# Early expert tiles chosen after four blocks instead of five, five of them instead of three, and the first expert weights loaded one block earlier

## The chip, the cores and the metric

One NeuronCore of a Trainium2 chip. The time is device microseconds from the start to the end of one execution. Five engines run their own instruction queues in order: TensorE (PE, with its weight loads as PEld), VectorE (DVE), ScalarE (ACT), GpSimd (POOL) and SyncE (SP, which here only issues DMAs).

## The reference

Three stages follow one another. A state-space attention over 4 x 8 sequences of 768 steps gives 3072 tokens of 256 values. A dense feed-forward layer (256 to 2048, leaky ReLU, back to 256) follows. Then each token goes to one of eight experts:

```
logits = x @ w_gate + modality_bias[modality_id]
e_idx = np.argmax(logits, axis=1)
...
gate_w = probs[np.arange(N), e_idx]
for e in range(E):
    mask = e_idx == e
    ...
    h = np.maximum(x[mask] @ w1[e], 0.0)
    out[mask] = gate_w[mask, None] * (h @ w2[e])
```

w1[e] and w2[e] hold 256 x 1024 and 1024 x 256 float32 values, 1 MB each. With the inputs that the reference draws, argmax gives all 3072 tokens to one expert: 2048 after four blocks of 512 tokens, 2560 after five. The dense layer's weights come as float64.

## The kernel before, in words

Every float32 matrix product is made of three fp32r products: each operand is split into a rounded part and a rest (hi, lo), and hi x hi, hi x lo and lo x hi are added. A split of weights is a cast on ACT and a subtraction on DVE or POOL (`split`, L531).

**Dense stage.** The tokens come in six blocks of 512. A block has 16 slots; in each, `mm1` makes one 128-row piece of the hidden layer (6 matmuls `h`), ACT, DVE, ACT, DVE make `sa`, `gg`, `gh`, `gl` from it, and `mm2` two slots later adds that piece to the block's output (6 matmuls `y`). Attention of later chunks, the conversion of the float64 weights (`load_win`, `load_wout`, `split_win`, `split_wout`, through the three 8 KB buffers of the pool `rawp`) and the routing of the block before are hung on slots with `at(slot, fn, ...)`. Slot 16j + f is piece f of block j, and L = 80 is the first slot of the last block (block 5). Offsets come from the dictionary Q.

**Routing.** For each block, three slots into the next one: `logits`, `ranks` (four indirect DMAs on POOL scatter the tokens' numbers into the list `il` in DRAM, ordered by expert), `rows` and `rows_out` (the block's output rows go to `yx` in DRAM). `ranks` also adds the block's counts to `base`.

**Expert stage.** It works in tiles of 256 tokens of one expert. For a tile, `m2_idx` (L802) reads its position from a table into an SP register, loads 256 token numbers (`gi`, a DMA on SP) and gathers their rows with two indirect DMAs on POOL (`xg`). `m2_w` (L790) reads the expert's number into an SP register and issues four DMAs of 512 KB on SP (r1: two halves of w1, L794; r2: two of w2, L797). `m2_split1` and `m2_split2` split r1 and r2 (four ACT casts; three DVE subtractions and one on POOL), `m2_xT` transposes and splits the gathered rows, `m2_mm1` makes `hp` (48 matmuls) and `hh`, `hl`, `m2_mm2` makes `o` (48 matmuls) and scatters the rows to the output (POOL).

The first EARLY = 3 tiles are taken from the counts after five blocks (`table_early`, L762, slot L + 5): only full tiles, so that later tokens change nothing in them. Their gathers read `yx` up to the start of the last block. The other tiles come from the final counts (`table_final`, L774), after the last block. 12 tiles run without condition; more stand under conditions that this input never meets.

**Buffers.** The attention's tiles and `rawp` are given back at slot L (`to_late`, L977). Only then are `raw2` (two r1, two r2, four xg) and `wp2` (the first tile's split weights) there.

**Order.** After the last block the list `fin` (L1006) holds: evict_y, logits, m2_xT(1), ranks, table_final, rows twice, m2_mm1(0), rows_out, m2_split1(1). Then for each tile i: m2_mm1(i), m2_xT(i+1), m2_split1(i+1), [m2_idx(i+2)], m2_w(i+2), m2_mm2(i), m2_split2(i+1); m2_idx stands there for tiles from EARLY on. A planner orders the instructions of each engine when the program is built, from its own estimate of when each can start (`schedule_with_timeline_sim=True`, L1070); instructions named in Q's 'pin' stay behind the instruction traced before them on their engine.

Of the kernel before, what the change touches and what calls it, by code (L numbers as in the profile page):

```python
# [8 lines left out]
F32 = mybir.dt.float32  # L9
# [15 lines left out]
Q = {'sg': (0, 1),  # L25
 'i00': 0,
 'i01': 1,
 'lo1': -1,
 'o00': 0,
 'o01': 4,  # L30
 'i10': 3,
 'i11': 3,
 'xe': 2,
# [11 lines left out]
 'rk': 3,  # L45
 'r0': 6,
 'r1': 6,
 'te': 5,
 'ix': 7,
 'w0': 5,  # L50
 'w1': 6,
 's1': 13,
 's2': 13,
 'xt': 14,
 'bt': 4,
 'cv': 2,
# [48 lines left out]
def kernel(  # L105
# [18 lines left out]
    NT, DM = out.shape  # L124
    DFF = w_in.shape[1]
    NE, _, F2 = w1.shape
    P = 128
    NCB = S // P
    NCH = NT // P
    NF = DFF // P  # L130
    NF2 = F2 // P
    T = 256
    KMAX = NT // T
    EARLY = 3
    NFIN = KMAX + NE - 1 - EARLY
    NSTAT = KMAX - EARLY
    YW = DM + 8
    W64 = w_in.dtype == mybir.dt.int64
    blocks = [(i * 512, 512) for i in range(NT // 512)]
# [4 lines left out]
    gp = ctx.enter_context(tc.tile_pool(name="gp", bufs=8))  # L144
    yp = ctx.enter_context(tc.tile_pool(name="yp", bufs=2))
    sp = ctx.enter_context(tc.tile_pool(name="sp", bufs=2))
    psh = ctx.enter_context(tc.tile_pool(name="psh", bufs=2, space=PSUM))
    psy = ctx.enter_context(tc.tile_pool(name="psy", bufs=2, space=PSUM))
    pscb = ctx.enter_context(tc.tile_pool(name="pscb", bufs=2, space=PSUM))
# [4 lines left out]

    early_ctx = ExitStack()
    ap_ = early_ctx.enter_context(tc.tile_pool(name="ap_", bufs=2))
    rawp = early_ctx.enter_context(tc.tile_pool(name="rawp", bufs=3))

    class Pinned:

# [65 lines left out]
    done = cst.tile([1, NE], F32, name="done")  # L226
    tabe = cst.tile([1, 2, EARLY], I32, name="tabe")
    tabf = cst.tile([1, 2, NFIN], I32, name="tabf")
# [506 lines left out]
    def pick(cum, m, tab, dn):  # L735
        sh = [1, m, NE]
        cb = cum.unsqueeze(1).to_broadcast(sh)
        le = sp.tile([1, NFIN, NE], F32, tag="le", name="le")[:, 0:m, :]
        v.tensor_tensor(out=le, in0=cb, in1=tio[:, 0:m].unsqueeze(2).to_broadcast(sh), op=ALU.is_le)
        et = sp.tile([1, NFIN], F32, tag="et", name="et")[:, 0:m]  # L740
        v.tensor_reduce(out=et, in_=le, axis=AX.X, op=ALU.add)
        v.tensor_scalar(out=et, in0=et, scalar1=float(NE - 1), scalar2=None, op0=ALU.min)
        v.tensor_tensor(out=le, in0=le, in1=cb, op=ALU.mult)
        kt = sp.tile([1, NFIN], F32, tag="kt", name="kt")[:, 0:m]
        v.tensor_reduce(out=kt, in_=le, axis=AX.X, op=ALU.max)
        v.tensor_tensor(out=kt, in0=tio[:, 0:m], in1=kt, op=ALU.subtract)
        if dn is not None:
            v.tensor_tensor(
                out=le, in0=ev[0:1].unsqueeze(1).to_broadcast(sh), in1=et.unsqueeze(2).to_broadcast(sh), op=ALU.is_equal
            )  # L750
            v.tensor_tensor(out=le, in0=le, in1=dn.unsqueeze(1).to_broadcast(sh), op=ALU.mult)
            dt = sp.tile([1, NFIN], F32, tag="dt", name="dt")[:, 0:m]
            v.tensor_reduce(out=dt, in_=le, axis=AX.X, op=ALU.add)
            v.tensor_tensor(out=kt, in0=kt, in1=dt, op=ALU.add)
        v.tensor_scalar(out=kt, in0=kt, scalar1=0.0, scalar2=float(KMAX - 1), op0=ALU.max, op1=ALU.min)
        vb = sp.tile([1, NFIN], F32, tag="vb", name="vb")[:, 0:m]
        v.tensor_scalar(out=vb, in0=et, scalar1=float(NT), scalar2=None, op0=ALU.mult)
        v.scalar_tensor_tensor(out=vb, in0=kt, scalar=float(T), in1=vb, op0=ALU.mult, op1=ALU.add)
        v.tensor_copy(tab[:, 0, :], et)
        v.tensor_copy(tab[:, 1, :], vb)  # L760

    def table_early():  # L762
# [6 lines left out]
        v.tensor_tensor(out=done, in0=nf, in1=cum, op=ALU.subtract)  # L769
        v.tensor_scalar(out=done, in0=done, scalar1=float(EARLY), scalar2=0.0, op0=ALU.add, op1=ALU.max)  # L770
        v.tensor_tensor(out=done, in0=done, in1=nf, op=ALU.min)
        pick(cum, EARLY, tabe, None)

# [14 lines left out]
    late = {}  # L788

    def m2_w(i, tab, k):  # L790
        ei = nc.values_load(tab[:, 0, k:k + 1], engines=[ENG.SP], min_val=0, max_val=NE - 1, skip_runtime_bounds_check_because=WHY)
        r1 = late["raw2"].tile([P, 2, F2], F32, tag="r1", name="r1")
        for k in range(2):
            nc.sync.dma_start(out=r1[:, k, :], in_=w1[bass.ds(ei, 1), k * P:(k + 1) * P, :].rearrange("o p f -> p (o f)"))  # L794
        r2 = late["raw2"].tile([P, NF2, DM], F32, tag="r2", name="r2")
        for k in range(2):
            nc.sync.dma_start(  # L797
                out=r2[:, 4 * k:4 * k + 4, :], in_=w2[bass.ds(ei, 1), k * 4 * P:(k + 1) * 4 * P, :].rearrange("o (k p) f -> p (o k) f", p=P)
            )
        m2.setdefault(i, {}).update(r1=r1, r2=r2)  # L800

    def m2_idx(i, tab, k):  # L802
        vi = nc.values_load(tab[:, 1, k:k + 1], engines=[ENG.SP], min_val=0, max_val=NE * NT - T, skip_runtime_bounds_check_because=WHY)
        gi = sp.tile([P, 2], I32, tag="gi", name="gi", bufs=6)
        r = nc.sync.dma_start(out=gi, in_=il[bass.ds(vi, T), :].rearrange("(q p) o -> p (q o)", p=P))
        for w in puts:
            tc.add_manual_dep(
                r.ins, w.name, mybir.DependencyInfo(mybir.DependencyClass.Sync, mybir.DependencyReason.DATA),
                reason="the list read here",
            )  # L810
        lim = blocks[-1][0] if tab is tabe else NT + 1
        xg = late["raw2"].tile([P, 2, YW], F32, tag="xg", name="xg", bufs=4)
        for q in range(2):
            g.indirect_dma_start(
                out=xg[:, q, :], out_offset=None, in_=yx[0:lim, :],
                in_offset=IndirectOffsetOnAxis(ap=gi[:, q:q + 1], axis=0), bounds_check=lim - 1, oob_is_err=False,
            )
        m2.setdefault(i, {}).update(gi=gi, xg=xg)
# [117 lines left out]
    def at(slot, fn, *args):  # L936
        sched.setdefault(max(slot, 0), []).append((fn, args))
# [37 lines left out]
    L = NF * (nb - 1)  # L975

    def to_late():  # L977
        early_ctx.close()
        late["wp2"] = ctx.enter_context(tc.tile_pool(name="wp2", bufs=2))
        late["raw2"] = ctx.enter_context(tc.tile_pool(name="raw2", bufs=2))  # L980

    at(L, to_late)
    at(L + Q["te"], table_early)
    for i in range(EARLY):
        at(L + Q["ix"], m2_idx, i, tabe, i)
    at(L + Q["w0"], m2_w, 0, tabe, 0)
    at(L + Q["w1"], m2_w, 1, tabe, 1)
    at(L + Q["s1"], m2_split1, 0)
    at(L + Q["s2"], m2_split2, 0)
    at(L + Q["xt"], m2_xT, 0)  # L990

    for j in range(nb):
# [20 lines left out]
    for i in range(len(tl)):  # L1013
        if i:
            run(m2_mm1, (i,), "L_")
            if i + 1 < len(tl):
                run(m2_xT, (i + 1,), "L_")
                run(m2_split1, (i + 1,), "L_")
        if i + 2 < len(tl):
            if i + 2 >= EARLY:  # L1020
                m2_idx(i + 2, *tl[i + 2])
            m2_w(i + 2, *tl[i + 2])
        run(m2_mm2, (i,), "L_" if i + 1 < len(tl) else "Z_")
        if i + 1 < len(tl):
            run(m2_split2, (i + 1,), "L_")
    u = nc.values_load(tabu, min_val=0, max_val=NFIN, skip_runtime_bounds_check_because=WHY)

    def cond(k):
        if k >= NFIN:
            return  # L1030
        with tc.If(u > k):
            i = EARLY + k
            m2_idx(i, tabf, k)
            m2_w(i, tabf, k)
            m2_split1(i)
            m2_split2(i)
            m2_xT(i)
            m2_mm1(i)
            m2_mm2(i)
            cond(k + 1)  # L1040
# [34 lines left out]
```

## Time and profile before

| | us |
|---|---|
| three timed runs | 578.73, 585.75, 586.8 |
| their median | 585.75 |
| the profiled execution's own time | 582.59 |
| its span, first to last instruction | 580.7 |
| PE busy | 535.6 (92%) |
| DVE, ACT, POOL busy | 366.2, 334.2, 196.8 |
| mean granted TensorE clock | 0.941 |

The rows further down come from the profiled execution. Times in them are microseconds from the start of its span. A granted clock of 1.00 is 2.4 GHz. "DMA share" is the mean busy share of the 16 DMA engines. In a chain of waits each piece is followed back to what released it. In a timeline row the bracket tells how long the engine stood idle before the instruction and what ended that.

### The profile page before, as it was taken

To read this page: it belongs to the slowest core of one execution; us is meant where nothing else is said; L and a number is where in the kernel's file an instruction comes from. 1 tells how busy PE (TensorE), PEld (TensorE's weight loads), DVE (VectorE), ACT (ScalarE), POOL (GpSimd) and SP (SyncE) were. 2 spreads that over 40 slices of the span, in tenths; PEclk is the share of its full clock that TensorE was granted. 3 is DMA by queue.
4 is the path that set the end of the run, shared out by engine and by line. 5 is a ranking of instruction groups with operands and counts; after the bars stand their busy time and mean duration, and the time that the engine had idled before them with its cause. 6 is when DMAs were issued, how large, how long until landed. Compare 5 with 4: busy or idle time off the path is not lost.

```text
span 580.7 us, 9512 instructions
## 1 busy us (share of the span) xinstructions
PE 535.6 (92%) x3411; PEld 430.4 (74%) x3411; DVE 366.2 (63%) x698; ACT 334.2 (58%) x699; POOL 196.8 (34%) x183
## 2 busy tenths in 40 slices
PE   6999959999999999999999999938987899999991
PEld 3435636678786878788778777826986899999991
DVE  6647998867667776775666665536575266645540
ACT  6427656766666686756765744334435367656640
POOL 5544787710201220013101100205063555456531
PEclk9558998999999999999999999989989799999996
DMA  8995630412243287322510100589008767676300
GB/s 196 143 249 126 189 109 5 100 11 54 34 93 85 46 51 97 78 32 25 119 46 2 39 1 1 21 192 297 20 22 187 251 217 230 225 234 219 114 20 21
DMA packets 128311, 61.01 MB, mean 105 GB/s; under 512 B 84545, under 2 KB 120514, under 8 KB 128258
## 3 DMA queue, kind: packets, MB, share of 16 engines
q1 hardware_dynamic: 125186, 53.94, 41.2%
q0 software_dynamic: 3072, 6.41, 3.3%
q8 instruction: 29, 0.48, 0.4%
q14 instruction: 24, 0.20, 0.2%
HBM read 53.73 MB, written 6.60 MB: 104 GB/s over the span
## 4 chain that ended last, share of the span: by engine, by line
PE 69%; issue 8%; DMA 8%; DVE 6%; POOL 4%; ACT 3%; POOLq 0%; SPq 0%; DVEq 0%; ACTq 0%
PE h L169 19%; PE y L169 18%; PE o L169 8%; PE hp L169 7%; PE psy L169 5%; PE cb L169 4%; DMA r<-in_moe_w_dram 3%; DMA il<-ids,pi 2%; DMA xg<-yx,gi 1%; PE bc L169 1%; DVE lb L169 1%; POOL out_dram L169 1%; PE ps L169 1%; DVE hb L169 1%; PE pb L169 1%
## 5 line engine op out<-in xcount | busy, mean ns | idle before, releaser
L169 ACT CAST gh<-gg 128x512 fp32r<-128x512 f32 x96 | 59.5, 620 | 65.5 <-DVE gg L169 65.4
L169 PE MATMUL h<-xh,wih 128*128 128x512 f32 x192 | 79.2, 416 | 10.6 <-DVE gg L169 10.4
L169 DVE TENSOR_TENSOR gl<-gg,gh 128x512 fp32r<-128x512 f32 x80 | 57.7, 721 | 41.4 <-ACT gh L169 41.2
L169 DVE TENSOR_TENSOR gg<-sa,h 128x512 f32<-128x512 f32 x96 | 65.5, 682 | 22.8 <-ACT sa L169 21.5
L169 PE MATMUL y<-gl,woh 128*128 128x512 f32 x192 | 77.9, 406 | 1.9 <-DVE gl L169 1.7
L169 PE MATMUL h<-xh,wil 128*128 128x512 f32 x192 | 76.4, 398 | 1.0 <-POOL wil L169 1.0
L169 PE MATMUL h<-xl,wih 128*128 128x512 f32 x192 | 76.5, 399 | 0.0
L169 POOL TENSOR_SCALAR_AFFINE_SELECT e<-e 128x1024 f32<-128x1024 f32 (+1 forms) x28 | 30.0, 1075 | 137.2 <-DMA e<-cumd 72.7
L169 PE MATMUL y<-gh,wol 128*128 128x512 f32 x192 | 76.3, 398 | 0.0
L169 PE MATMUL hp<-x2h,w1s 128*128 128x256 f32 x384 | 72.6, 286 | 0.0
L169 PE MATMUL o<-w2s,hh 128*128 128x256 f32 x384 | 71.1, 290 | 0.0
L169 PE MATMUL y<-gh,woh 128*128 128x512 f32 x192 | 65.0, 406 | 5.4 <-ACT gh L169 5.4
L169 ACT ACTIVATE sa<-h 128x512 f32<-128x512 f32 x96 | 57.2, 595 | 21.1 <-PE h L169 18.3
L169 DVE SCALAR_TENSOR_TENSOR hl<-hp,hh 128x512 fp32r<-128x512 f32 x48 | 33.2, 691 | 54.5 <-ACT hh L169 52.4
L169 PEld LDWEIGHTS hp<-x2h,w1s 128*128 128x128 f32 x384 | 61.9, 195 | 0.1
L169 PEld LDWEIGHTS o<-w2s,hh 128*128 128x128 f32 x384 | 60.1, 197 | 0.0
L169 POOL DMA_INDIRECT il<-ids,pi x24 | 25.0, 1040 | 101.2 <-DVE pi L169 50.4
L169 PE MATMUL hp<-x2l,w1s 128*128 128x256 f32 x192 | 54.2, 288 | 0.0
L169 PEld LDWEIGHTS h<-xh,wih 128*128 128x128 f32 x192 | 36.7, 192 | 23.0 <-DVE gg L169 14.0
L169 ACT ACTIVATE hh<-hp 128x512 fp32r<-128x512 f32 x48 | 28.6, 598 | 41.7 <-PE hp L169 36.3
L169 PE MATMUL o<-w2s,hl 128*128 128x256 f32 x192 | 51.9, 287 | 0.0
L169 ACT ACTIVATE e<-e,ncum 128x128 f32<-128x128 f32 x160 | 51.2, 395 | 0.0
(206 smaller groups left out, 1035.5 us busy)
## 6 DMA issues: line engine op xcount, KB each, us to landing
r<-in_moe_w_dram SPq DMA_DIRECT2D x48, 512.0 KB, 5.2
e<-cumd SPq DMA_DIRECT2D x20, 512.0 KB, 7.6
raw<-in_moe_w_in_dram SPq DMA_DIRECT2D x4, 1024.0 KB, 5.5
raw<-in_moe_w_out_dram SPq DMA_DIRECT2D x4, 1024.0 KB
yx<-ysb SPq DMA_DIRECT2D x6, 528.0 KB
xt<-in_x_dram SPq DMA_DIRECT2D x24, 128.0 KB, 4.0
ct<-in_C_dram SPq DMA_DIRECT2D x24, 64.0 KB, 4.6
bt<-in_B_dram SPq DMA_DIRECT2D x24, 64.0 KB
```

The lines of the kernel that those rows point to most:

```text
L169: r = f(*args, **kw)
```

## The change

It does the following.

- EARLY goes from 3 to 5. The two tables change size with it: tabe holds 5 tiles, tabf 14 instead of 16; 12 tiles still run without condition (5 + 7).
- `table_early` and `m2_w` of tile 0 move from slot L + 5 to slot L - 16 + 3 + 1 = 68, in block 4, right behind `ranks` of block 3. The early table is so made from four blocks' counts, and the early gathers read `yx` only up to the start of block 4's rows (`blocks[-2]`).
- The pool `rawp` lives to the end. r1 and r2 no longer have buffers of their own (two each in raw2) but take turns in rawp's three. r1 of tile i + 2 so waits for the split of r2 of tile i, and r2 of tile i + 2 for the split of r1 of tile i + 1; before, r1 and r2 of tile i + 2 waited for the split of r1 and of r2 of tile i.
- `m2_idx` of the early tiles (five now) moves from slot L + 7 to L + 1. xg gets six buffers instead of four.
- The split of tile 0's r1 moves from L + 13 to L + 4, that of r2 from L + 13 to L + 6. `m2_w` of tile 1 moves from L + 6 to L + 9. `m2_xT` of tile 0 stays at L + 14.

```diff
@@
- 'te': 5,
- 'ix': 7,
- 'w0': 5,
- 'w1': 6,
- 's1': 13,
- 's2': 13,
@@
-    EARLY = 3
+    EARLY = 5
@@
+    rawp = ctx.enter_context(tc.tile_pool(name="rawp", bufs=3))
@@
-    rawp = early_ctx.enter_context(tc.tile_pool(name="rawp", bufs=3))
@@ def m2_w(i, tab, k):
-        r1 = late["raw2"].tile([P, 2, F2], F32, tag="r1", name="r1")
+        r1 = rawp.tile([P, 2, F2], F32, tag="raw", name="r1")
...
-        r2 = late["raw2"].tile([P, NF2, DM], F32, tag="r2", name="r2")
+        r2 = rawp.tile([P, NF2, DM], F32, tag="raw", name="r2")
@@ def m2_idx(i, tab, k):
-        lim = blocks[-1][0] if tab is tabe else NT + 1
-        xg = late["raw2"].tile([P, 2, YW], F32, tag="xg", name="xg", bufs=4)
+        lim = blocks[-2][0] if tab is tabe else NT + 1
+        xg = late["raw2"].tile([P, 2, YW], F32, tag="xg", name="xg", bufs=6)
@@
+    at(L - NF + Q["rk"] + 1, table_early)
+    at(L - NF + Q["rk"] + 1, m2_w, 0, tabe, 0)
     at(L, to_late)
-    at(L + Q["te"], table_early)
     for i in range(EARLY):
-        at(L + Q["ix"], m2_idx, i, tabe, i)
-    at(L + Q["w0"], m2_w, 0, tabe, 0)
-    at(L + Q["w1"], m2_w, 1, tabe, 1)
-    at(L + Q["s1"], m2_split1, 0)
-    at(L + Q["s2"], m2_split2, 0)
+        at(L + 1, m2_idx, i, tabe, i)
+    at(L + 4, m2_split1, 0)
+    at(L + 6, m2_split2, 0)
+    at(L + 9, m2_w, 1, tabe, 1)
     at(L + Q["xt"], m2_xT, 0)
```

## Rows read from the trace of the kernel before

**Rows 1.** The page: PE's busy tenths in 40 slices of 14.5 us.

```profile
PE   6999959999999999999999999938987899999991
```

**Rows 2.** Busy by stretch: us, PE, PEld, DVE, ACT, POOL, granted clock, DMA share, GB/s.

```profile
300.00:360.00 60.00, 60.00 (x366) 47.14 (x355) 38.22 (x86) 34.30 (x77) 4.23 (x4) 1.00 0.04 10
...
378.00:396.30 18.30, 7.59 (x18) 4.78 (x19) 7.91 (x7) 7.15 (x10) 2.36 (x1) 0.81 0.90 233
...
423.50:431.00 7.50, 5.93 (x43) 5.64 (x43) 5.85 (x23) 1.66 (x3) 6.12 (x6) 0.77 0.10 35
...
452.50:457.50 5.00, 4.95 (x24) 4.98 (x25) 0.00 (x0) 0.41 (x1) 2.04 (x2) 0.50 1.05 372
457.50:545.00 87.50, 87.50 (x732) 87.50 (x732) 52.21 (x60) 57.19 (x83) 47.73 (x36) 1.00 0.66 213
```

**Rows 3.** The chain that ended last (start, us, what).

```profile
372.60 18.50 DMA r<-in_moe_w_dram
...
396.46 1.36 PE h L169 x6
...
431.79 9.12 DMA il<-ids,pi
...
444.79 7.62 DMA xg<-yx,gi
...
461.30 5.76 PE hp L169 x48
...
473.24 5.76 PE hp L169 x48
479.44 5.76 PE o L169 x48
```

**Rows 4.** SP's timeline around the first expert weights.

```profile
370.43 0.72 SPq L794 DMA_DIRECT2D r<-in_moe_w_dram  x2
...
434.50 0.37 SPq L724 DMA_DIRECT2D yx<-ysb  x1
```

**Rows 5.** ACT's timeline: first and last cast of tile 0's split.

```profile
381.25 1.04 ACT L169 CAST w1s<-r 128x1024 fp32r<-128x1024 f32 x1 [8.58 <-DMA r<-in_moe_w_dram]
...
391.12 1.05 ACT L169 CAST w2s<-r 128x1024 fp32r<-128x1024 f32 x1 [1.31 <-DMA r<-in_moe_w_dram]
```

**Rows 6.** PE's timeline: the first hp matmul of tile 2.

```profile
440.00 0.28 PE L169 MATMUL hp<-x2h,w1s 128*128 128x256 f32 x1
```

**Rows 7.** DVE's timeline: first and last of table_early's 18 instructions.

```profile
365.48 0.24 DVE L169 TENSOR_TENSOR cm<-base,thr 1x96 f32<-1x96 f32 x1
...
370.77 0.16 DVE L169 CAST tabe<-vb 1x3 int32<-1x3 f32 x1
```

**Rows 8.** POOL's and DVE's timelines: POOL's part of tile 0's split, and `gl`.

```profile
392.31 2.36 POOL L169 TENSOR_TENSOR w2s<-r,w2s 128x1024 fp32r<-128x1024 f32 x1 [20.47 <-DMA r<-in_moe_w_dram]
...
392.72 2.50 DVE L169 TENSOR_TENSOR gl<-gg,gh 128x512 fp32r<-128x512 f32 x1 [1.65 <-ACT gh L169]
...
396.50 0.69 DVE L169 TENSOR_TENSOR gl<-gg,gh 128x512 fp32r<-128x512 f32 x1 [0.69 <-ACT gh L169]
```

**Rows 9.** Timelines of SP, DVE, POOL and ACT in the even part of the expert stage.

```profile
465.67 0.98 SPq L797 DMA_DIRECT2D r<-in_moe_w_dram  x2
467.60 0.38 SPq L805 DMA_DIRECT2D gi<-il  x1
...
469.14 2.36 DVE L169 TENSOR_TENSOR w1s<-r,w1s 128x1024 fp32r<-128x1024 f32 x2
...
472.84 1.05 POOL L169 DMA_INDIRECT xg<-yx,gi  x1 [4.68 <-DMA gi<-il]
...
475.24 2.40 POOL L169 TENSOR_TENSOR w2s<-r,w2s 128x1024 fp32r<-128x1024 f32 x1
...
481.89 2.01 ACT L169 CAST w2s<-r 128x1024 fp32r<-128x1024 f32 x2
```

**Rows 10.** The tile r (raw expert weights): time of its 48 DMAs from issue to landing.

```profile
DMA to landing us min/median/max: 3.8/5.2/19.0
```

## The prediction

> **What bounds the kernel now.** I read the page's slices first. PE is at 9 tenths almost everywhere; the reader is to see the 3 in the 27th slice (377 to 392 us) and the 8, 9, 8, 7, 8 behind it [rows 1]. PE sets the time, and what can be won cheaply lies where it stands still. The busy times by stretch show how still: in 300 to 360 PE is busy 60.00 of 60 us at clock 1.00, in 457.5 to 545 it is busy 87.50 of 87.50; from 378.0 to 396.3 it has 18 matmuls in 18.3 us, and the stretches from 423.5 and 452.5 run at granted clocks of 0.77 and 0.50 [rows 2]. The chain that ended last says what PE waited for: a DMA of expert weights for 18.50 us from 372.60, and later the list's scatter (9.12 us from 431.79) and the gather (7.62 us from 444.79) [rows 3].
>
> *First hole.* SP issues the weights of tiles 0 and 1, 4 MB, one behind the other from 370.43 [rows 4]. ACT stands in front of tile 0's first cast until 381.25 and begins the last at 391.12 [rows 5]; the dense stage's `sa` and `gh` are queued behind these casts, and PE behind them. Six matmuls take 1.36 us at the even pace [rows 3], so the 18 in this stretch need 4.1 us: 18.3 - 4.1 = **14.2 us lost**.
>
> *Second hole.* Tile 3 is the first from the final table. `m2_mm1` of tile 2 begins at 440.00 [rows 6], that of tile 3 at 461.30, that of tile 4 at 473.24 [rows 3]. An even tile is 473.24 - 461.30 = 11.94 us; from tile 2 to tile 3 it is 21.3. **9.4 us lost**, partly idle, partly at the clock of 0.50 (1.2 of 2.4 GHz) that PE has from 452.5, when it resumes [rows 2].
>
> *A third dent*, 423.5 to 431: 7.50 - 5.93 = 1.57 us idle and a clock of 0.77 [rows 2], at most 1.57 + 0.23 x 7.5 = 3.3 us. There block 5's routing is mixed with tile 1's split.
>
> **The change part by part.** *Weights of tile 0, slot L + 5 to 68.* The register read and four DMAs (2 MB) move 17 slots ahead, at least 17 x 2 x 1.36 = 46 us, so from 370.43 to about 325 on SP [rows 4]. On SP's queue they pass block 4's `rows_out` and the early gi loads; none of these waits for them. The DMA share in 300 to 360 is 0.04 [rows 2], and 2 MB is half of what took 18.5 us, so they land by about 336. The split at L + 4 and L + 6 comes some 7 slots (20 us) ahead of the old hole, near 355. The 14.2 us go; next in line there is PE itself, as in the stretches beside it. If the cover were gone (weights issued as late as 345), ACT would wait again, a few us.
>
> *table_early with it.* 18 small DVE instructions, from 365.48 to 370.77 between others [rows 7], some 3 us of work, move from block 5 into block 4. There DVE has 38.2 of 60 us busy and PE never waits [rows 2]. Bounds 0 to 3; I take 0.
>
> *Tile 0's split at L + 4 and L + 6.* Four casts of 1.05, three DVE subtractions of 1.2, one on POOL of 2.36, during which `gl` on DVE takes 2.50 instead of 0.69 [rows 5, 8]. They now fall among running slots, beside logits, ranks and rows of block 4. The two slots between `mm1` and `mm2` are 4 x 1.36 = 5.4 us for a chain of four instructions of some 0.7 us [rows 8], so about 2.5 us of delay at a time are hidden. Bounds 0 (all hidden) and 6 (4.2 of casts and 1.8 of `gl` shown in full); I take +1.0, near the lower, since block 4 carries as much for attention (ACT 34.3, DVE 38.2 of 60) at no cost [rows 2].
>
> *m2_idx of five tiles at L + 1.* Five gi DMAs on SP, ten gathers on POOL, two in 2.4 us [rows 9], ahead of block 4's four scatters. The rows and list entries they read are those of blocks 0 to 3, written long before. POOL has 4.2 of 60 us busy [rows 2]; nothing waits for the scatters behind them until table time. Cost 0, at most a delay of those scatters by 12 us, which their list, read after the last block, has to spare.
>
> *m2_w of tile 1, L + 6 to L + 9.* Four DMAs behind `rows_out` of block 4. w1 goes into the third buffer, w2 waits for the split of tile 0's r1. Its split comes only after the last block, behind m2_mm1(0), some 30 us later; five times the landing time [rows 10]. Cost 0.
>
> *Five early tiles.* Tiles 3 and 4 need no final table. Tile 5 does, 2 x 11.94 = 24 us later than tile 3 did, where 9.4 were lost, so those go. Next late is tile 5's gather: gi is read behind tile 4's w2, gathered some 10 us later and lands 5 to 8 us ahead of its transposes.
>
> *Three weight buffers instead of four: the added wait.* In the even part w1's split ends at 469.14 + 2.36 = 471.5; w2's DMAs of the next tile now go out there. Before, w2 went 12 us earlier, at 465.67 for a cast at 481.89 [rows 9]. With 0.9 us to issue and 5.2 to land [rows 10] it is there at 477.6, 4 us early. Behind this wait on SP stand the next gi and w1: gi moves from 467.60 to about 473.4, so its gather on POOL, which started 5.24 us after it, from 472.84 to about 478.7 [rows 9]. The trace shows no such loop. From below 0 (POOL's subtraction goes first: casts end near 472, gather after it, 24 us ahead of use; PE full). From above: the gather keeps its place ahead of the subtraction, which then ends near 483.5 instead of 477.6 [rows 9], while `o` starts at 479.44 [rows 3] and needs it after 12 of its matmuls, at 480.9: 2.6 us for each of seven gathered tiles, 18 us. I take 0: the planner's order follows readiness, and the casts are ready 6 us before the gather would be. The same order decides for tile 2's w2. Should it stand behind block 5's `rows_out` (434.50 [rows 4], 420.3 without the first hole), it lands at 420.3 + 0.9 + 5.2 = 426.4 [rows 9, 10]. Tile 2's `hp` is due at 440.00 - 14.2 = 425.8 [rows 6] and the cast of w2 some 3 us before (481.89 against `hp` near 485.2, after the 48 `o` from 479.44 [rows 3, 9]): 3 to 4 us late.
>
> *Third dent.* Its program order is not touched; I leave it. Bounds: gain 3.3, loss 0.
>
> *Smaller tables, six xg buffers:* 0.
>
> Sum: 580.7 - 14.2 - 9.4 + 1.0 = 558.1 us span, and 1.9 around it (582.59 - 580.7): 560.0. The profiled execution lies 3.2 under the median of the runs and 1.2 under their mean (583.8), so I add 1: **561 us**, 3.7% under the profiled time.
>
> **The rivals.**
>
> *A: the tile loop waits, clock kept (11%).* Both holes go, but each gathered tile waits 2.6 us at POOL's subtraction: 560 + 18 = 578. For it: gather ahead of subtraction is POOL's order now [rows 9]. Against: that order came from a gi ready early, and in the change it is not.
>
> *B: the same loop with the clock (7%), slower than before.* In the dent 1.57 us of idling go with a granted clock of 0.77 over 7.5 us [rows 2], 1.7 us more. If every wait of 2.6 brought some 2 us of low clock, seven tiles cost 7 x 4.6 = 32: 592, slower by 1.6%. It outweighs the two holes from a wait of about 3.4 us per tile in all. The Trainium skill ("TensorE: Matmul & The Clock Gate", "HAM oscillation — how this bites in real kernels") describes this form: a kernel that waits once in every tile starts each tile at the low clock. [...]
>
> *C: one hole in part (10%).* Tile 2's w2 behind `rows_out`: 3 to 4 us idle and as much at the low clock, 567. That the change fails to do what it says (weights still late in block 5) would leave 560 + 14 = 574; I see no way to it but an SP queue held until 345, and count it here.
>
> *Forecast (72%):* both holes gone, 553 to 567.
>
> **How the numbers follow.** A measurement of this kernel tells about 2% from no change, so faster means under 571. Forecast and C are faster: 0.82. A is within 2%, and of B 0.04: 0.15. The rest of B, with a dearer wait, is slower by over 2%: 0.03. Range: from 552 (the dent gone too, 560 - 3.3, and runs 4 us under the profile as the lowest was) to 578, which holds C and half of A.
>
> **What would show it.** r's DMAs from L794 near 320 to 330, ten gathers near 350 to 365; ACT's casts `w1s` without a wait for r; PE full at clock 1.00 from 378 to 396; no `xps` waiting for `xg`; an even tile still 11.94 us from `hp` to `hp`. Wrong if `o` or PEld waits for POOL's `w2s` in each tile, if ACT waits for r in the expert stage, or if PE in block 5 shows idle time before `y` for `gh` or `gl`.

## The result and the profile after

| | before | after |
|---|---|---|
| runs side by side, us | 578.73, 585.75, 586.8, 583.09 | 558.4, 560.86, 562.31, 562.98 |
| their median | 584.42 | 561.59 |
| profiled execution's own time | 582.59 | 558.4 |
| its span | 580.7 | 556.7 |
| mean granted TensorE clock | 0.941 | 0.966 |

The ratio is 0.9615, with a 95% interval of 0.9531 to 0.9699: faster, by 3.9%. The ratios, here and in the table of experiments, leave out runs that fell in a slower state of the chip (one of early3's four, some of the runs of before); the medians hold all runs. The 561 forecast lies 0.6 below the median. The profiled execution of after is the fastest of its four runs, so a few of the 24.0 us between the two profiles are not the change's; they are found below.

In the code of after the helper that records every instruction is L163 (L169 before), and SP issues r1, r2, gi and the block's rows from L788, L791, L799 and L718 (L794, L797, L805 and L724 before).

The page of after, PE's busy tenths in 40 slices:

```profile
PE   7979959999999999999999999999989999999991
```

The 3 of [rows 1] is gone; what is left of the sag is one 8 in the 30th slice. The same table by stretch as in [rows 2], of after:

```profile
300.00:360.00 60.00, 60.00 (x347) 47.63 (x346) 40.45 (x103) 33.76 (x74) 14.13 (x14) 1.00 0.50 100
...
378.00:396.30 18.30, 18.30 (x95) 15.57 (x95) 9.39 (x14) 7.59 (x13) 0.00 (x0) 1.00 0.37 64
...
405.00:420.00 15.00, 12.38 (x98) 12.08 (x97) 11.69 (x41) 5.32 (x10) 9.29 (x7) 0.89 0.68 179
...
420.00:520.00 100.00, 100.00 (x840) 100.00 (x839) 60.01 (x72) 64.85 (x94) 54.36 (x39) 1.00 0.72 212
```

From 378 to 396.3 PE has 95 matmuls where it had 18 [rows 2], at clock 1.00. From 420 on it is never idle: the second hole is gone as well. One dent remains, 405 to 420: 2.62 us idle, and a granted clock of 0.89.

The chain that ended last shows the even pace of the tiles. In after it holds no DMA of expert weights any more; the `hp` of tiles 2 and 3 are:

```profile
425.27 5.76 PE hp L163 x48
...
437.22 5.76 PE hp L163 x48
```

They are 11.95 us apart; before, it was 21.1 (440.00 [rows 6] to 461.13, the first `hp` of tile 3 in PE's timeline).

How the weights came: SP's and ACT's timelines of after.

```profile
317.70 0.98 SPq L788 DMA_DIRECT2D r<-in_moe_w_dram  x2
319.44 2.38 SPq L791 DMA_DIRECT2D r<-in_moe_w_dram  x2
335.38 4.28 SPq L799 DMA_DIRECT2D gi<-il  x5
...
340.61 2.00 ACT L163 CAST w1s<-r 128x1024 fp32r<-128x1024 f32 x2
...
371.63 2.00 ACT L163 CAST w2s<-r 128x1024 fp32r<-128x1024 f32 x2
```

The four DMAs of tile 0 go out at 317.70 and 319.44 instead of 370.43 [rows 4], and neither cast has a bracket: ACT waits for no weight, where it stood 8.58 us in [rows 5]. The planner put the casts of w1 at 340.61, still in block 4, ahead of the slot that the program names (L + 4).

**Where the 24.0 us of the two spans came from.** Two landmarks of ACT's timeline divide the span: the copy `yt` that empties block 4's output, and the cast `x2h` that ends tile 2's transposes. First before, then after:

```profile
351.77 0.58 ACT L169 COPY yt<-y 128x512 f32<-128x512 f32 x1
...
435.40 0.59 ACT L169 CAST x2h<-xps 128x512 fp32r<-128x512 f32 x1
```

```profile
348.35 0.58 ACT L163 COPY yt<-y 128x512 f32<-128x512 f32 x1
...
420.52 0.59 ACT L163 CAST x2h<-xps 128x512 fp32r<-128x512 f32 x1 [0.74 <-PE xps L163]
```

Up to block 4's `yt` after is 3.4 us ahead; 3.2 of these stand already at block 0's `yt` (120.02 against 123.21), where the engines' orders are the same in both kernels. Over the twelve profiles of this study that landmark lies between 118.5 and 123.4, whatever the kernel: this is spread, not the change. From `yt` to `x2h` it took 83.6 us before and 72.2 after: 11.4 less. From `x2h` to the end it took 145.3 and 136.2: 9.1 less. So the change is worth 20.6 in the profiles (24.0 - 3.4) and 22.8 in the medians.

### The profile page after: what moved, and what is told of

Same layout as the page of the kernel before. It is cut to its first block, busy times and chain, and to the rows that moved or that the text cites. A ratio compares the mean times of both kernels' runs of the same rounds, so it can differ in the third digit from the quotient of the medians.

```text
span 556.7 us, 9530 instructions
## 1 busy us (share of the span) xinstructions
PE 524.3 (94%) x3411; PEld 426.7 (77%) x3411; DVE 367.7 (66%) x698; ACT 333.4 (60%) x699; POOL 200.3 (36%) x183
## 4 chain that ended last, share of the span: by engine, by line
PE 77%; DVE 6%; issue 4%; ACT 4%; POOL 4%; DMA 2%; SPq 2%; another core or an unknown queue 0%; POOLq 0%; DVEq 0%; ACTq 0%
PE y L163 21%; PE h L163 21%; PE hp L163 12%; PE o L163 10%; PE psy L163 4%; PE cb L163 3%; DMA ct<-in_C_dram 1%; PE pc L163 1%; PE yr L163 1%; DVE lb L163 1%; PE pb L163 1%; ACT e L163 1%; PE xps L163 1%; SPq L358 1%; POOL gl L163 1%
## 5 line engine op out<-in xcount | busy, mean ns | idle before, releaser
L163 ACT CAST gh<-gg 128x512 fp32r<-128x512 f32 x96 | 59.6, 620 | 69.2 <-DVE gg L163 64.5
L163 PE MATMUL h<-xh,wih 128*128 128x512 f32 x192 | 79.5, 418 | 7.2 <-DVE gg L163 7.1
L163 DVE TENSOR_TENSOR gl<-gg,gh 128x512 fp32r<-128x512 f32 x80 | 57.5, 719 | 39.1 <-ACT gh L163 37.8
L163 DVE TENSOR_TENSOR gg<-sa,h 128x512 f32<-128x512 f32 x96 | 65.4, 681 | 23.4 <-ACT sa L163 21.7
L163 POOL TENSOR_SCALAR_AFFINE_SELECT e<-e 128x1024 f32<-128x1024 f32 (+1 forms) x28 | 29.3, 1048 | 138.9 <-DMA e<-cumd 90.3
L163 PE MATMUL h<-xh,wil 128*128 128x512 f32 x192 | 76.8, 400 | 1.0 <-POOL wil L163 1.0
L163 PE MATMUL y<-gl,woh 128*128 128x512 f32 x192 | 77.2, 402 | 0.4 <-POOL gl L163 0.2
L163 PE MATMUL h<-xl,wih 128*128 128x512 f32 x192 | 77.1, 401 | 0.0
L163 PE MATMUL y<-gh,wol 128*128 128x512 f32 x192 | 75.7, 394 | 0.0
L163 PE MATMUL hp<-x2h,w1s 128*128 128x256 f32 x384 | 73.3, 286 | 0.0
L163 ACT ACTIVATE sa<-h 128x512 f32<-128x512 f32 x96 | 57.2, 596 | 22.8 <-PE h L163 17.8
L163 PE MATMUL o<-w2s,hh 128*128 128x256 f32 x384 | 69.3, 285 | 0.0
L163 DVE SCALAR_TENSOR_TENSOR hl<-hp,hh 128x512 fp32r<-128x512 f32 x48 | 33.0, 691 | 52.8 <-ACT hh L163 39.4
L163 PE MATMUL y<-gh,woh 128*128 128x512 f32 x192 | 64.1, 399 | 0.0
L163 PEld LDWEIGHTS hp<-x2h,w1s 128*128 128x128 f32 x384 | 62.3, 195 | 0.6
L163 POOL TENSOR_TENSOR w2s<-r,w2s 128x1024 fp32r<-128x1024 f32 x12 | 33.5, 2789 | 73.5 <-ACT w2s L163 42.8
L163 PEld LDWEIGHTS o<-w2s,hh 128*128 128x128 f32 x384 | 58.4, 191 | 0.4 <-issue 0.4
L163 PE MATMUL hp<-x2l,w1s 128*128 128x256 f32 x192 | 54.2, 287 | 0.0
L163 ACT ACTIVATE hh<-hp 128x512 fp32r<-128x512 f32 x48 | 28.5, 597 | 42.5 <-PE hp L163 36.1
L163 ACT ACTIVATE e<-e,ncum 128x128 f32<-128x128 f32 x160 | 51.3, 395 | 3.8 <-POOL e L163 3.8
L163 PEld LDWEIGHTS h<-xh,wih 128*128 128x128 f32 x192 | 36.8, 192 | 18.8 <-DVE gg L163 10.9
L163 PE MATMUL o<-w2s,hl 128*128 128x256 f32 x192 | 51.1, 283 | 0.0
```

Source lines behind the costliest of these rows:

```text
L163: r = f(*args, **kw)
```

## The experiments

Kernels of one group below ran beside the same runs of before. The two landmarks give a measure for each that the spread ahead of them doesn't touch. There is spread behind the work too: from the last scatter on POOL to the end of the span it took 11.3 to 13.2 us, with no relation to the edits (11.5 in before and in after, 13.1 in five_only, 13.2 in routing_first). So the second measure ends at that scatter, in POOL's timeline of after this one:

```profile
545.17 0.98 POOL L163 DMA_INDIRECT out_dram<-o,gi  x1 [0.34 <-ACT o L163]
```

All stretches are in us, from the profiles; after and before stand for comparison:

| kernel | `yt` of block 4 to `x2h` of tile 2 | `x2h` of tile 2 to the last scatter | median | ratio to before (95%) |
|---|---|---|---|---|
| before | 83.6 | 133.84 | 584.42 | 1 |
| after | 72.2 | 124.65 | 561.59 | 0.9615 (0.9531 to 0.9699) |
| early3 | 70.6 | 133.21 | 567.34 | 0.9656 (0.9590 to 0.9723) |
| five_only | 87.9 | 124.65 | 579.12 | 0.9869 (0.9819 to 0.9919) |
| four_buffers | 70.6 | 124.65 | 560.53 | 0.9556 (0.9517 to 0.9594) |
| weights_late | 68.2 | 125.99 | 559.21 | 0.9532 (0.9483 to 0.9582) |
| routing_first | 66.1 | 124.66 | 555.67 | 0.9503 (0.9464 to 0.9542) |
| gather_first | 65.3 | 155.92 | 585.66 | 1.0050 (1.0012 to 1.0087) |
| weights_held | 74.9 | 124.65 | 565.31 | 0.9701 (0.9623 to 0.9779) |
| table_five | 84.0 | 124.66 | 573.78 | 0.9854 (0.9783 to 0.9924) |
| gather_first_four | 65.3 | 143.52 | 570.31 | 0.9792 (0.9714 to 0.9869) |
| routing_first_slots | 67.6 | 124.64 | 557.29 | 0.9582 (0.9516 to 0.9648) |

Against the times expected beforehand (quoted below), four_buffers came out inside its range, routing_first 1.3 us under it, and table_five and routing_first_slots 0.3 or less outside. early3, five_only, gather_first, weights_held and gather_first_four fell between their two ranges, so for them the landmarks and waits have to decide. weights_late contradicted its theory.

### Group 1: which part takes which hole

**early3**: after, with three early tiles.

```diff
-    EARLY = 5
+    EARLY = 3
```

> The changed kernel with EARLY = 3 (the only edit): weights, gathers and table stay early, but tile 3 comes from the final table again. Theory (the second hole is the wait for the final table's list and gather): xps of tile 3 waits for xg, tile 2 to tile 3 takes some 21 us from hp to hp instead of 11.95, and the time is 561.6 + 9 = 570 to 572. Rival (the second hole went because weights and gathers of the first tiles came earlier, and the number of early tiles is idle): 561 to 563, with 12 us from hp to hp.

The second hole is back: 133.2 us from tile 2's `x2h` to the last scatter, 8.6 more than after. The chain and PE's timeline of early3 show the same links as before [rows 3], the list's scatter and the gather:

```profile
413.33 9.33 DMA il<-ids,pi
...
427.75 6.37 DMA xg<-yx,gi
...
433.32 0.45 PE L163 MATMUL xps<-ident,xg 128*128 128x128 f32 x1 [5.22 <-DMA xg<-yx,gi]
```

The bracket shows PE idle for 5.22 us. By the whole time the step is less clear (0.9656 against 0.9615, some 2.4 us, and the two intervals overlap); the landmarks, which leave out the spread ahead of them, tell it.

**five_only**: before, with five early tiles and six gather buffers, everything else left.

```diff
-    EARLY = 3
+    EARLY = 5
...
-        xg = late["raw2"].tile([P, 2, YW], F32, tag="xg", name="xg", bufs=4)
+        xg = late["raw2"].tile([P, 2, YW], F32, tag="xg", name="xg", bufs=6)
```

> The kernel before with EARLY = 5 and six xg buffers, all else as before. Theory (the two holes are apart and add up): the second hole goes (12 us from hp of tile 2 to hp of tile 3), the first stays (PE loses some 14 us near 378 to 396): 584 - 9 = 574 to 576. Rival (five early tiles need the other edits): 582 or more.

The second hole goes alone (124.65, as in after), the first stays, and is 4.3 us longer (87.9). ACT's first cast waits for its weights as before:

```profile
381.89 1.04 ACT L169 CAST w1s<-r 128x1024 fp32r<-128x1024 f32 x1 [9.60 <-DMA r<-in_moe_w_dram]
```

SP now issues five gi loads behind the weights, and tile 0's `x2h` comes at 412.4 instead of 408.3. So the count of early tiles is worth 8.6 to 9.2 us by itself, and the two parts of the change don't lean on each other, except that five early tiles cost something where the weights are late.

**four_buffers**: after, with a fourth buffer, for r2 of odd tiles.

```diff
-        r2 = rawp.tile([P, NF2, DM], F32, tag="raw", name="r2")
+        odd = i % 2 == 1
+        r2 = (late["raw2"].tile([P, NF2, DM], F32, tag="rx", name="r2", bufs=1) if odd
+              else rawp.tile([P, NF2, DM], F32, tag="raw", name="r2"))
```

> The changed kernel with a fourth weight buffer for r2 of the odd tiles, which gives back the waits of before (r1 and r2 of tile i + 2 wait for the splits of r1 and r2 of tile i). Theory (the three buffers cost nothing, since w2 lands some 4 us ahead of its cast): 561.6 within 2, and 11.95 us from hp to hp as in the changed kernel. Rival (they cost a wait in each tile or at tile 1): 2 to 6 us faster.

124.65 in both: a fourth buffer gives nothing, so the added wait of three costs nothing as the planner orders it. SP's waits in after between 430 and 520 show it as a queue's idling that nobody feels:

```profile
SPq L791 <- DVE w1s L163: 56.1, 8, 8.5
SPq L788 <- POOL w2s L163: 4.8, 7, 0.9
```

The columns are the sum, the times, the longest. r2 waits for DVE, long but early; the wait for POOL is 0.9 us at most. And POOL takes its subtraction ahead of the gather, as POOL's timeline of after shows for one tile:

```profile
449.42 2.81 POOL L163 TENSOR_TENSOR w2s<-r,w2s 128x1024 fp32r<-128x1024 f32 x1 [5.28 <-issue]
...
455.20 1.05 POOL L163 DMA_INDIRECT xg<-yx,gi  x1 [0.46 <-issue]
```

In four_buffers POOL has the other order from tile 3 on: it gathers first and subtracts behind that. PE waits for nothing there either. POOL's timeline of four_buffers for one tile:

```profile
449.85 1.05 POOL L163 DMA_INDIRECT xg<-yx,gi  x1 [4.68 <-DMA gi<-il]
...
452.25 2.42 POOL L163 TENSOR_TENSOR w2s<-r,w2s 128x1024 fp32r<-128x1024 f32 x1
```

So with four buffers and the splits where after has them, either order on POOL is free.

**weights_late**: after, with the loads and splits of the weights back in block 5's slots and only the table left in block 4.

```diff
-    at(L - NF + Q["rk"] + 1, m2_w, 0, tabe, 0)
...
-    at(L + 4, m2_split1, 0)
-    at(L + 6, m2_split2, 0)
-    at(L + 9, m2_w, 1, tabe, 1)
+    at(L + 5, m2_w, 0, tabe, 0)
+    at(L + 6, m2_w, 1, tabe, 1)
+    at(L + 13, m2_split1, 0)
+    at(L + 13, m2_split2, 0)
```

> The changed kernel with the weights of tiles 0 and 1 issued at L + 5 and L + 6 and tile 0's splits at L + 13, as before the change; table, gathers, five tiles and three buffers stay. Theory (the first hole is ACT standing in front of casts whose weights land late): ACT's first w1s cast waits for r again, PE stops in block 5, and the time is 561.6 + 8 to 14 = 570 to 576. Rival (the earlier table and gathers took the first hole away): 561 to 564.

A miss: 559.21, no slower than after. The edit did not make the weights late. SP's and ACT's timelines of weights_late:

```profile
335.03 0.89 SPq L788 DMA_DIRECT2D r<-in_moe_w_dram  x2
...
344.47 2.00 ACT L163 CAST w1s<-r 128x1024 fp32r<-128x1024 f32 x2
346.36 2.00 ACT L163 CAST w2s<-r 128x1024 fp32r<-128x1024 f32 x2
```

The planner issued them at 335.03, 17 us later than in after but some 35 us ahead of where before had them, and put all four casts at the end of block 4. So the slots that the program names for the weights move the loads within block 4 and are worth no time here; what may decide is when the numbers they need, the table's, are there. Two runs of group 3 test that.

### Group 2: the remaining dent, and the order that the prediction feared

**routing_first**: after, with both w2 subtractions of tile 1 on DVE, and queued there behind the last block's routing (`ohb`) and tile 1's `x2l`.

```diff
-    def split(raw, hi, lo, eng):
+    def split(raw, hi, lo, eng, behind=None):
...
+        for m in behind or ():
+            tc.add_manual_dep(
+                r.ins, m.name, mybir.DependencyInfo(mybir.DependencyClass.NoSync, mybir.DependencyReason.DATA),
...
-            split(d["r2"][:, ks, :], d["w2"][:, ks, 0, :], d["w2"][:, ks, 1, :], v if k == 0 else g)
+            split(d["r2"][:, ks, :], d["w2"][:, ks, 0, :], d["w2"][:, ks, 1, :], v if k == 0 or i == 1 else g, mark["x2l"] if i == 1 else None)
```

> The changed kernel with both subtractions of tile 1's w2 on DVE, queued behind ohb of the last block's routing and x2l of tile 1. Theory (the dent that is left near 408 to 417 is DVE held at w2s by POOL's own w2s, with the routing and x2l queued behind it): PE's wait of 2.1 us for ohb and 0.5 for x2l goes and so does the low clock behind it, 2 to 4 us: 557 to 560. Rival (PE waits for the routing's own length): the wait at rp stays above 1.5 us and the time is 561 to 563.

The dent of after, on PE, DVE and POOL in its timelines:

```profile
404.80 2.81 POOL L163 TENSOR_TENSOR w2s<-r,w2s 128x1024 fp32r<-128x1024 f32 x1 [28.60 <-ACT w2s L163]
...
405.29 3.41 DVE L163 TENSOR_TENSOR w2s<-r,w2s 128x1024 fp32r<-128x1024 f32 x1
...
410.12 0.18 DVE L163 CAST ohb<-oh 128x32 bf16<-128x32 f32 x1
...
410.36 0.19 PE L163 MATMUL rp<-ohb,tris 128*128 128x32 bf16 x1 [2.11 <-DVE ohb L163]
411.24 0.65 PE L163 MATMUL yr<-ident,yt 128*128 128x128 f32 x4 [0.52 <-DVE x2l L163]
```

DVE's subtraction takes 3.41 us beside POOL's, where it takes 1.22 elsewhere; block 5's routing stands behind it on DVE, and PE waits 2.11 us for the routing's `ohb`. In routing_first the order is turned (DVE's timeline), and the stretch is full (busy by stretch):

```profile
409.10 0.18 DVE L163 CAST ohb<-oh 128x32 bf16<-128x32 f32 x1
409.36 0.66 DVE L163 TENSOR_TENSOR x2l<-xps,x2h 128x512 fp32r<-128x512 f32 x1
409.94 2.35 DVE L163 TENSOR_TENSOR w2s<-r,w2s 128x1024 fp32r<-128x1024 f32 x2
```

```profile
405.00:420.00 15.00, 15.00 (x135) 14.96 (x134) 13.65 (x42) 8.86 (x15) 6.57 (x6) 1.00 0.78 192
```

15.00 of 15.00 at clock 1.00, against 12.38 at 0.89 in after: 2.62 idle and 0.11 x 15 = 1.65 of clock, 4.3 us, which agrees with 70.6 - 66.1 = 4.5 against four_buffers, which has the same dent. Its ratio, 0.9503, is the lowest measured here. It is faster than before; that it is faster than after rests on the landmarks, since the two intervals overlap a little (0.9531 to 0.9542). The edit does two things, it takes POOL's part away and queues the subtractions behind the routing; which of them it takes was not separated.

**gather_first**: after, with the w2 split moved behind the list load and gather of the tile two later, its POOL part pinned there, so that POOL gathers first. It was meant to measure the upper bound of the three buffers' wait. It moves more than that: the whole w2 split of every tile, with its casts on ACT and its subtraction on DVE, stands one tile later in the program.

```diff
+         'G_m2_split2': 'g',
...
+        if EARLY <= i + 2 < len(tl):
+            m2_idx(i + 2, *tl[i + 2])
+        if i:
+            run(m2_split2, (i,), "G_" if EARLY <= i + 2 < len(tl) else "L_")
         if i + 2 < len(tl):
-            if i + 2 >= EARLY:
-                m2_idx(i + 2, *tl[i + 2])
             m2_w(i + 2, *tl[i + 2])
         run(m2_mm2, (i,), "L_" if i + 1 < len(tl) else "Z_")
-        if i + 1 < len(tl):
-            run(m2_split2, (i + 1,), "L_")
```

> The changed kernel with POOL's subtraction of each tile's w2 queued behind the gather of the tile two later, for the seven tiles from the final table (the order in which POOL stood before the change). It measures the loop of rivals A and B. A: some 2.6 us of waiting at o in each of the seven tiles at an unchanged clock, 561.6 + 18 = 578 to 582. B: the clock falls as well, 588 to 596. If the loop costs nothing (my slack was too small): 561 to 564.

Nothing of the gain is left: 585.66, the interval just above 1. Up to tile 2's `x2h` it takes 65.3, since tile 1's w2 subtractions, and with them the dent and tile 1's `o`, come behind that landmark; from there to the last scatter it takes 155.9 against 124.7 in routing_first. Over both stretches that is 30.4 more, and its median is 30.0 above that of routing_first. Waits of SP, PE, ACT and POOL in gather_first, 430 to 520:

```profile
SPq L792 <- POOL w2s L164: 16.3, 5, 5.0
...
PE xps L164 <- DVE x2l L164: 7.8, 3, 4.6
PE o L164 <- ACT hh L164: 5.2, 1, 5.2
...
ACT w1s L164 <- DMA r<-in_moe_w_dram: 18.8, 4, 9.3
...
POOL xg L164 <- DMA gi<-il: 25.8, 5, 6.6
```

There is a ring in it. SP's r2 waits for POOL's subtraction (5 times), the next gi and r1 stand behind it in SP's queue, POOL's gather waits for gi and ACT's cast for r1, and POOL's next subtraction comes behind that gather. PE's own waits are mostly for DVE's `x2l` and ACT's `hh` (13.0 of 15.5 us), engines that the late casts hold up; none is for POOL. PE pays in idling and in clock; busy by stretch of gather_first, over the stretch that is full in after:

```profile
420.00:520.00 100.00, 84.53 (x666) 83.03 (x666) 44.75 (x51) 47.78 (x71) 42.10 (x29) 0.93 0.62 178
```

15.5 us idle in 100, and 7 more at a clock of 0.93.

But POOL's order is not what starts the loss. ACT casts tile 1's w2 only at 418.41 (402.72 in after), and POOL's subtraction of tile 1, which no gather from the final table precedes, stands waiting for that cast (POOL's timeline of gather_first):

```profile
420.51 2.87 POOL L164 TENSOR_TENSOR w2s<-r,w2s 128x1024 fp32r<-128x1024 f32 x1 [5.02 <-ACT w2s L164]
```

PE waits 8.7 us (1.73, 5.19 and 1.80 in its timeline) ahead of 447.81, where POOL begins the first gather from the final table. The loads also wait for other splits than in after: mostly r1 for DVE's `w1s` and r2 for POOL's `w2s`, the other way round. So the 30 us belong to the later split and the order on POOL together; what gathering first alone would cost with three buffers no run shows.

### Group 3: table or weights, and what a fourth buffer repairs

**weights_held**: after, with tile 0's weights queued on SP behind block 4's rows, and the splits at L + 13. The table stays in block 4.

```diff
+            if i == 0:
+                tc.add_manual_dep(
+                    r.ins, sent_rows[-1].name, mybir.DependencyInfo(mybir.DependencyClass.NoSync, mybir.DependencyReason.DATA),
...
-    at(L - NF + Q["rk"] + 1, m2_w, 0, tabe, 0)
...
-    at(L + 4, m2_split1, 0)
-    at(L + 6, m2_split2, 0)
+    at(L + 7, m2_w, 0, tabe, 0)
     at(L + 9, m2_w, 1, tabe, 1)
+    at(L + 13, m2_split1, 0)
+    at(L + 13, m2_split2, 0)
```

> The changed kernel with tile 0's weight DMAs queued on SP behind rows_out of block 4 and tile 0's splits at L + 13: table, gathers, five tiles and three buffers stay early, the weights alone are late (the run with the later slots did not delay them, since the planner issued them as soon as the table was there). Theory (the first hole is ACT standing in front of casts whose weights land late): the weights go out near 370, ACT's w1s cast waits for r, PE stops in block 5, 570 to 576. Rival (what took the hole away is something else in the early table): 560 to 564.

SP, ACT and PE in its timelines:

```profile
373.07 1.01 SPq L790 DMA_DIRECT2D r<-in_moe_w_dram  x2
...
383.87 1.04 ACT L163 CAST w1s<-r 128x1024 fp32r<-128x1024 f32 x1 [7.99 <-DMA r<-in_moe_w_dram]
...
385.94 0.70 PE L163 MATMUL hp<-x2h,w1s 128*128 128x256 f32 x2 [4.85 <-ACT x2h L163]
```

ACT waits 7.99 us for weights that go out as late as before had them, and PE stands idle behind it: the mechanism is the predicted one. The landmarks alone understate the price (74.9 - 70.6 = 4.3 us against four_buffers), because the dent is in the 70.6 and mostly gone here. Busy by stretch of weights_held tells the two apart, the hole and the dent:

```profile
375.00:395.00 20.00, 14.96 (x72) 12.18 (x71) 10.28 (x11) 7.60 (x11) 2.57 (x1) 0.91 0.94 251
...
407.00:421.00 14.00, 12.77 (x114) 11.29 (x113) 10.74 (x36) 7.95 (x14) 6.97 (x5) 1.00 0.52 170
```

The hole is 5.04 us idle and 0.09 x 20 = 1.8 of clock, 6.8 us, about half of the 14.2; the dent is 1.23 us idle at a clock of 1.00. Of the four casts (383.87 to 389.2) only the first waits: when ACT comes to w2, at 386.72, it has landed.

**table_five**: after, with the early table from five blocks again (slots as before the change); five early tiles and three buffers stay.

```diff
-    at(L - NF + Q["rk"] + 1, table_early)
-    at(L - NF + Q["rk"] + 1, m2_w, 0, tabe, 0)
     at(L, to_late)
+    at(L + 5, table_early)
...
-        lim = blocks[-2][0] if tab is tabe else NT + 1
+        lim = blocks[-1][0] if tab is tabe else NT + 1
...
```

> The changed kernel with the early table from five blocks again: table_early and tile 0's weights at L + 5, tile 1's at L + 6, gathers at L + 7 with rows up to the last block, splits at L + 13; five tiles and three buffers stay. Theory (the count of four blocks is what lets the weights go out in block 4; the slots alone do nothing): weights go out near 370, the first hole is back in full, 574 to 580, as in the run with five tiles alone (579). Rival (three buffers in place of four spread the 4 MB and shorten the hole): 566 to 570.

The first hole is back in full (84.0, before 83.6), and the second stays away (124.66). ACT and PE in its timelines:

```profile
378.71 1.04 ACT L163 CAST w1s<-r 128x1024 fp32r<-128x1024 f32 x1 [7.90 <-DMA r<-in_moe_w_dram]
...
386.99 1.04 ACT L163 CAST w2s<-r 128x1024 fp32r<-128x1024 f32 x1 [4.79 <-DMA r<-in_moe_w_dram]
...
380.81 0.87 PE L163 MATMUL y<-gh,woh 128*128 128x512 f32 x2 [4.72 <-ACT gh L163]
389.95 1.22 PE L163 MATMUL y<-gh,woh 128*128 128x512 f32 x2 [4.20 <-ACT gh L163]
```

Here w2 has not landed when ACT comes to it, so each pair of casts waits for its own DMA, with the dense stage's `gh` behind both: two waits, two idle stretches of PE, much as in [rows 5]. w2's first half came 17.4 us after its issue (369.56); in weights_held it was there after at most 12.5 (374.26 to 386.72). What made it later here was not separated.

**gather_first_four**: gather_first with the fourth buffer of four_buffers (both edits stand above).

> The kernel with POOL's gathers ahead of its subtractions, with a fourth weight buffer (r2 of the odd tiles). Theory (the three buffers are free only because POOL subtracts before it gathers; with four, either order is free): most of the 24 us of the gather-first run goes, 560 to 566. Rival (the gather-first order costs by itself, through POOL's lateness at o): 578 or more.

570.31: over both stretches 208.8, so the buffer gives back 12.4 of gather_first's 30.4 (by the ratios 15). The rest, 18.0, is not POOL's order by itself, as the rival had it: four_buffers has that order, with four buffers, at no cost. It stays with what else the edit moves, the later w2 split; which wait makes it was not separated. So late weights for want of a buffer are one part of gather_first's loss and not the whole.

**routing_first_slots**: routing_first with the weights' slots of weights_late (both edits stand above).

> Both edits that came out faster than the changed kernel or equal to it: the last block's routing ahead of tile 1's w2 subtractions, and the later slots for tile 0's and tile 1's weights and splits, after which the planner casts all of tile 0's weights at the end of block 4. If they add up: 553 to 555; if the second did nothing beyond the spread of runs: 555 to 557, as routing first alone (555.7).

0.9582 against 0.9503, the intervals overlapping: nothing is added. weights_late by itself had little of the dent left (0.88 us idle from 405 to 420, at a clock of 1.00), so the two take mostly the same thing.

## Why the prediction was right

**First hole.** The cause was right: in weights_held and table_five, ACT stands in front of late weights with the dense stage's instructions queued behind it, and PE behind those; without the change's table nothing of the 14.2 is won. The size is shown in part: late weights alone bring back 6.8 of it, the rest only together with a late table and late gathers. The measured gain on this stretch was 11.4. The difference is the dent's growth (3.3 at most before by the sum in the prediction, 4.3 by the same reckoning in after: 1.0) and 1.28 us of idle PE that no other kernel here shows (the paragraph on crowding); that leaves 0.5 for the crowding, for which I had taken 1.0.

**What carried it.** The prediction put the gain down to the moved slot of tile 0's weights. weights_late shows that this slot is worth nothing: with the old slot the loads still go out in block 4 (335.03), and with the table back in block 5 they go out at 368.44 (table_five). It is the four-block table that lets them go early. The instruction that decides was taken for one that costs up to 3 us and brings nothing.

**Crowding in block 4 and 5.** Taken +1.0. In the profiled execution PE waits once more than the sum has it:

```profile
361.74 0.60 ACT L163 ACTIVATE sa<-h 128x512 f32<-128x512 f32 x1 [1.31 <-remote]
...
363.12 0.50 PE L163 MATMUL h<-xh,wih 128*128 128x512 f32 x1 [1.28 <-DVE gg L163]
```

These are ACT's and PE's timelines of after. What held ACT for 1.31 us the trace does not name. early3 and four_buffers, with the same order there, are 1.6 us shorter between the two landmarks, so I count it as this execution's; its cause is open. The table (taken 0) and the ten gathers (taken 0) cost nothing: PE has 60.00 of 60 us from 300 to 360.

**Second hole.** Predicted 9.4, with tile 2's start from PE's timeline (440.00) and tile 3's from the chain (461.30); with both from the timeline (461.13) it is 9.2. That is what came: 9.2 from `hp` to `hp` in after, 9.2 done alone (five_only), 8.6 undone alone (early3).

**Three buffers.** Taken 0, since the planner would take POOL's subtraction first. It did, and the fourth buffer of four_buffers is worth nothing. The other order with three buffers was not measured by itself, so neither the upper bound of 18 nor the choice between A and B is settled. gather_first costs 30 us, clock included, but it moves the whole w2 split along. The waits in it are not those of the prediction either: PE does not wait in each tile at `o` for POOL's subtraction, but mostly through ACT, whose casts come late or wait for r1 held up in SP's queue.

**Tile 2's w2 behind the rows** (rival C): it did not happen. SP issued that w2 at 405.40, ahead of block 5's rows (417.57), and `hp` of tile 2 starts at 425.27 without a wait.

**Third dent.** Left alone in the sum. It stayed, 1.0 us larger, because in after POOL's w2 subtraction of tile 1 starts ahead of DVE's. Before, DVE was first, and its subtraction kept its 1.22 us (timelines of DVE and POOL, before):

```profile
421.68 1.22 DVE L169 TENSOR_TENSOR w2s<-r,w2s 128x1024 fp32r<-128x1024 f32 x1
...
421.99 3.15 POOL L169 TENSOR_TENSOR w2s<-r,w2s 128x1024 fp32r<-128x1024 f32 x1 [14.72 <-ACT w2s L169]
```

PE waited for the routing there too, 1.27 us for `ohb` against 2.11 in after. DVE is first also in weights_late (407.22 against 407.63), weights_held (411.61 against 412.01) and table_five (421.71 against 422.02), where the dent is 0.9 to 1.5 us idle at a clock of 1.00.

**The sum.** 560.0 in the sum and 561 forecast; 561.59 in the median, 558.4 in the profile. The profile is lower by the 3.4 that the spread ahead of block 4 gave it; without these it would stand at 561.8, 1.8 above the sum: 1.0 of dent, 1.3 of the unnamed wait and 0.3 behind tile 2's `x2h` (9.1 where 9.4 was forecast), less the 0.5 of crowding that did not come and 0.2 around the span. That 561 came within 0.6 of the median is luck in part: the interval of the ratio is some 10 us wide, and the 1 us that was added for the spread of runs made up for half of what the sum missed.

## What to carry to other kernels

Where a planner orders the queues by readiness, ask which value makes a load ready; here moving the call changed no time, making the value earlier did. When buffers are cut down, write out the ring that the new wait closes (queue, engine, queue), and test it with a run that moves one instruction and nothing else: gather_first moved a whole split, lost 30 us, more than the change gains, and can't say which part of the move lost them. And pin what is short and needed at once (the routing) ahead of what is long and not yet needed (a weight split) on the same engine.

## What the runs showed of the hardware

DVE's subtraction of 128x1024 from SBUF took 1.22 us, and 3.41 when POOL's like subtraction had started 0.5 us before it. The subtraction ended about 1.1 us after POOL's end (408.70 against 407.61), as if it had not run until then. `gl` took 2.57 in after (at 374.18) instead of 0.69 beside one. The Trainium skill says this in "SBUF — State Buffer", "Who interferes with whom": a DVE instruction with two inputs in SBUF contends with a GpSimd instruction that reads SBUF, the port pair they share is an exclusive lock, and the order of issue decides which of them is blocked. The rows agree with that in both orders: in before, POOL came second, and its instruction took 3.15 instead of 2.36 [rows 8].

The first 120 us, with the same order of instructions in every kernel here, took between 118.5 and 123.4 us from one execution to the next: a fifth of the gain measured, and the reason to compare profiles by landmarks inside the span.
